# An attention and SwiGLU kernel on one core: a reordered opening, crossbar transposes of queries and keys from batch 2 on, values loaded uncast by SyncE, and one normalisation over two PSUM banks

## The chip, the cores and the metric

The kernel runs on one core of one Trainium2 chip. The metric is device time in microseconds (us), the median of several executions. The profile is one execution of the same program; its span is about two microseconds shorter than that execution's device time (424.5 us of 426.5 before).

Engines are named as in the profile: PE is TensorE, DVE VectorE, ACT ScalarE, POOL GpSimd (Pool), SP SyncE. "SPq" marks the time in which SyncE's sequencer is occupied with issuing a DMA.

## The reference, cut to what matters

```python
# q, k, v: (8 batches, 8 heads, 576 rows, 64); global_idx: 8 row numbers
scores = q @ k^T / sqrt(64)
mask   = (|i - j| <= 32) | row i is global | row j is global
x      = softmax(where(mask, scores, -1e9)) @ v       # -> (4608, 512)
g      = x @ w_gate                                   # (512, 1536)
out    = (g * sigmoid(g) * (x @ w_val)) @ w_out       # (4608, 512), float32
```

## The kernel before

The feed-forward part (FFN) works through nine chunks of 512 rows, which are numbered 0 to 8 here. A chunk is 12 gates (two PSUM tiles of four matmuls each, 128x512) and four output steps of 12 matmuls: 144 matmuls. The attention of batch c+1 is cut into steps that are issued between the gates of chunk c. So batch 0 runs alone at the start, chunks 0 to 6 carry the attention of batches 1 to 7, and chunks 7 and 8 are bare.

Four parts matter here. First, every batch's queries and keys are transposed by TensorE through PSUM and copied out by ACT and DVE. (Cuts are marked `...`.)

```python
def step_T(hp):                       # four of these per batch
    ...
    for name in ("k", "q"):
        ps = pm.tile([P, LJ, LP], BF16, tag="m", name="ps_t")     # pm: 2 tiles of one bank
        for j in range(LJ):
            for par in range(2):
                nc.tensor.transpose(out=ps[64*par : 64*par+64, j, :], ...)
        if name == "k": nc.scalar.copy(out=kT[:, hp, ...], in_=...)
        else:           nc.vector.tensor_copy(out=st["qT"][:, hp, :]..., in_=...)
```

Second, the values. Pool's DMAs cast them from float32 to bfloat16 on the way into `va`. SyncE then copies them within SBUF into `vb`, a version shifted by 64 rows, which half of the matmuls of the attention's second product ("AV") read.

```python
def load_v(b):
    for u in range(5):
        ...
        nc.gpsimd.dma_start(out=va[lo:hi, u, :, 0:D], in_=vs[t0 + lo : t0 + hi])

def load_vb(b):
    vb = bp.tile([P, 4, H, W], BF16, tag="vb", name="vb")
    nc.sync.dma_start(out=vb[0:64], in_=va[64:128, 0:4])
    nc.sync.dma_start(out=vb[64:128], in_=va[0:64, 1:5])
```

Third, the AV tiles: each pair of row tiles has two head groups, and each head group is one PSUM tile that DVE normalises by itself.

```python
def step_AV(u):
    for tp in (t0 // 2, t0 // 2 + 1):
        ps = pm.tile([P, 4, W], FP32, tag="m", name="ps_av")
        ...                                            # 10 matmuls, va and vb in turn
        normalise(ps, st["xa", tp][:, 4*hg : 4*hg+4, :])   # reduce, reciprocal, multiply
```

Fourth, the order. The gathered global rows are masked by Pool into `kqm` (`gather`, `gather_mask`); `kqm` is transposed by `step_GT`. The loop ties one attention step to each FFN unit, and the loads of batch c+2 to the third gate of chunk c.

```python
[L(step_T, 0), L(step_GT)], [L(step_T, 1)], [L(step_T, 2), vb], [L(step_T, 3)],
[L(step_S2)], [L(step_SG)], [L(step_P2T), L(step_S, 0)], [L(step_S, 1), L(step_AV2)],
[L(step_S, 2), L(step_AV, 0)], [L(step_S, 3), L(step_AV, 1)],
[L(step_X, 0), L(step_X, 1), L(step_S, 4)], [L(step_AV, 2)], [L(step_AV, 3)],
[L(step_X, 2), L(step_X, 3)], [L(step_AV8)], [L(step_X8)],
...
for c in range(NCH):
    steps = attention(c + 1) if c + 1 < B else []
    for i, f in enumerate(ffn(c)):
        f()
        for g in steps[i] ...: g()
        if i == 2 and c + 2 < B: prefetch(c + 2)     # gather, q and k, values, kqm
```

The softmax here doesn't subtract the row's maximum and nothing guards it: scores larger than these inputs give would overflow.

Of the kernel before, what the change touches and what calls it, by code (L numbers as in the profile page):

```python
# [26 lines left out]
def kernel(  # L27
# [22 lines left out]
    NCH = NT // CH  # L50
# [11 lines left out]
    ldp = ctx.enter_context(tc.tile_pool(name="ldp", bufs=2))  # L62
# [7 lines left out]
    pm = ctx.enter_context(tc.tile_pool(name="pm", bufs=2, space=bass.MemoryType.PSUM))  # L70
# [3 lines left out]
    def load_qk_part(b, tiles, hg):  # L74
        for name, src in (("k", k), ("q", q)):
            nc.gpsimd.dma_start(  # L76
                out=tiles[name][:, 4 * hg : 4 * hg + 4, :],
                in_=src[b, 4 * hg : 4 * hg + 4].rearrange("h (p j) d -> p h (j d)", j=LJ),
            )
# [6 lines left out]
    va_bufs = [const.tile([P, 5, H, W], BF16, name=f"va{i}") for i in range(2)]  # L86

    def load_v(b):
        va = va_bufs[b % 2]
        vs = v[b].rearrange("h s d -> s h d")  # L90
        for u in range(5):
            lo = WIN if u == 0 else 0
            hi = P - WIN if u == 4 else P
            t0 = P * u - WIN
            nc.gpsimd.dma_start(out=va[lo:hi, u, :, 0:D], in_=vs[t0 + lo : t0 + hi])  # L95

    def load_vb(b):
# [11 lines left out]
    load_qk_part(0, loaded[0], 0)  # L109
# [4 lines left out]
    iq_i = const.tile([P, KC], I32)  # L114
    nc.gpsimd.iota(iq_i, pattern=[[1, KC]], base=-WIN, channel_multiplier=0)
    load_qk_part(0, loaded[0], 1)
    i8_i = const.tile([P, NG], I32)
    nc.gpsimd.iota(i8_i, pattern=[[1, NG]], base=0, channel_multiplier=0)
    bofs_i = const.tile([P, B], I32)
    nc.gpsimd.iota(bofs_i, pattern=[[H * S, B]], base=0, channel_multiplier=0)  # L120
    band = const.tile([P, 64], BF16)
    nc.gpsimd.memset(band, 1.0)
    nc.gpsimd.affine_select(
        out=band, in_=band, compare_op=ALU.is_ge, fill=0.0,
        base=0, pattern=[[-1, 64]], channel_multiplier=1,
    )
    nc.gpsimd.affine_select(
        out=band, in_=band, compare_op=ALU.is_ge, fill=0.0,
        base=2 * WIN, pattern=[[1, 64]], channel_multiplier=-1,
    )  # L130
    for i in range(2):
        nc.gpsimd.memset(va_bufs[i][:, :, :, D : D + 2], 0.0)
        nc.gpsimd.memset(va_bufs[i][:, :, :, D : D + 1], 1.0)
        nc.gpsimd.memset(va_bufs[i][0:WIN, 0, :, :], 0.0)
        nc.gpsimd.memset(va_bufs[i][P - WIN : P, 4, :, :], 0.0)


    gidx_f = const.tile([P, NG], FP32)
    nc.vector.tensor_copy(
        out=gidx_f, in_=gidx_i64.bitcast(I32).rearrange("p (a b) -> p a b", b=2)[:, :, 0]  # L140
# [4 lines left out]
    )  # L145
    tmp8 = const.tile([P, NG], FP32)
# [3 lines left out]
    oh16 = const.tile([P, HP, 2, 2], FP32)  # L150
    nc.vector.tensor_reduce(
        out=oh16.rearrange("p h a r -> p (h a r)"),
        in_=ident.rearrange("p (a g) -> p a g", g=NG), axis=AX.X, op=ALU.add,
    )
    dmask = const.tile([P, HP, 2], FP32)
    nc.vector.tensor_tensor(out=dmask, in0=oh16[:, :, 0, :], in1=oh16[:, :, 1, :], op=ALU.add)
    mka = const.tile([P, 2, 2], FP32)
    nc.vector.tensor_reduce(
        out=mka, in_=oh16.rearrange("p h a r -> p a r h"), axis=AX.X, op=ALU.add
    )  # L160
    asel = const.tile([P, 2], FP32)
    nc.vector.tensor_reduce(out=asel, in_=mka, axis=AX.X, op=ALU.add)
    i8_f = const.tile([P, NG], FP32)
    nc.vector.tensor_copy(out=i8_f, in_=i8_i)
# [9 lines left out]
    bofs_f = const.tile([P, B], FP32)  # L174
    nc.vector.tensor_copy(out=bofs_f, in_=bofs_i)
    nc.vector.tensor_scalar(out=gofs, in0=bofs_f, scalar1=hrow, scalar2=None, op0=ALU.add)

# [21 lines left out]
    kqms = [None] * B  # L199
    g0 = gather(0)  # L200
    load_v(0)
    kqms[0] = gather_mask(*g0)

# [13 lines left out]
    for i in range(3):  # L217
        load_wgv(i)


    iq = const.tile([P, KC], FP32)
    nc.vector.tensor_copy(out=iq, in_=iq_i)
    nc.vector.tensor_scalar(out=iq, in0=iq, scalar1=gcol, scalar2=None, op0=ALU.subtract)
    m1 = const.tile([P, KC], BF16)
    nc.vector.tensor_scalar(out=m1, in0=iq, scalar1=0.0, scalar2=None, op0=ALU.is_equal)
    m0 = const.tile([P, KC], BF16)
    nc.vector.tensor_tensor(out=iq, in0=iq, in1=iq, op=ALU.mult)
    nc.vector.tensor_scalar(
        out=m0, in0=iq, scalar1=(WIN + 0.5) ** 2, scalar2=None, op0=ALU.is_gt
    )  # L230
    ones = const.tile([P, P], BF16)
    nc.vector.memset(ones, 1.0)
    ps_i = psc.tile([P, 2, 512], FP32, tag="sc", name="ps_i")
    for i in range(2):
        nc.tensor.matmul(
            out=ps_i[:, i, 0:320], lhsT=ones, rhs=m1[:, 320 * i : 320 * (i + 1)],
            start=True, stop=True,
        )
    mg = const.tile([P, S], BF16)
    mt = const.tile([P, KC], BF16)  # L240
    nc.vector.tensor_scalar(
        out=mg, in0=m0[:, WIN : WIN + S], scalar1=asel[:, 0:1], scalar2=None, op0=ALU.mult
    )
    nc.vector.scalar_tensor_tensor(
        out=mg, in0=m1[:, WIN : WIN + S], scalar=asel[:, 1:2], in1=mg,
        op0=ALU.mult, op1=ALU.add,
    )
    mg2 = const.tile([P, KC], BF16)
    nc.vector.scalar_tensor_tensor(
        out=mt.rearrange("p (i c) -> p i c", i=2), in0=ps_i[:, :, 0:320], scalar=0.5,  # L250
        in1=m0.rearrange("p (i c) -> p i c", i=2), op0=ALU.is_lt, op1=ALU.mult,
    )
    nc.vector.tensor_scalar(
        out=mt, in0=mt, scalar1=asel[:, 1:2], scalar2=None, op0=ALU.mult
    )
    nc.vector.memset(mt[:, 0:WIN], 0.0)
    nc.vector.memset(mt[:, WIN + S : KC], 0.0)
    nc.vector.scalar_tensor_tensor(
        out=mg2, in0=m1, scalar=asel[:, 0:1], in1=mt, op0=ALU.mult, op1=ALU.add,
    )  # L260

    kT_bufs = [const.tile([P, HP, KC], BF16, name=f"kT{i}") for i in range(2)]
    for i in range(2):
        nc.vector.memset(kT_bufs[i][:, :, 0:WIN], 0.0)
        nc.vector.memset(kT_bufs[i][:, :, WIN + S : KC], 0.0)


    def attention(b):
# [4 lines left out]

        def step_T(hp):
            if hp == 0:
                st["qT"] = bp.tile([P, HP, S], BF16, tag="qT", name="qT")
            for name in ("k", "q"):
                ps = pm.tile([P, LJ, LP], BF16, tag="m", name="ps_t")
# [8 lines left out]
                if name == "k":  # L287
                    nc.scalar.copy(  # L288
                        out=kT[:, hp, WIN : WIN + S].rearrange("p (i j) -> p i j", j=LJ),
                        in_=ps.rearrange("p j i -> p i j"),  # L290
                    )
                else:
                    nc.vector.tensor_copy(  # L293
                        out=st["qT"][:, hp, :].rearrange("p (i j) -> p i j", j=LJ),
                        in_=ps.rearrange("p j i -> p i j"),
                    )

        def step_GT():
            kqm = kqms[b]
            ps = pm.tile([P, 2, P], BF16, tag="m", name="ps_g")  # L300
# [8 lines left out]
        def step_SG():  # L309
            ps = psc.tile([P, 2, 512], FP32, tag="sc", name="ps_sg")  # L310
            for i in range(2):
                for hp in range(HP):
# [3 lines left out]
                        rhs=st["qT"][:, hp, 288 * i : 288 * (i + 1)],  # L316
# [28 lines left out]
        def step_P2T():  # L345
            ps = pm.tile([P, 5, P], BF16, tag="m", name="ps_p2t")
# [7 lines left out]
        def step_AV2():  # L354
            ps = pm.tile([P, 2, W], FP32, tag="m", name="ps_av2")
# [22 lines left out]
        def step_S(u):  # L378
# [6 lines left out]
            for slot, hp, t in slots:  # L385
                for par in range(2):
# [4 lines left out]
                        rhs=st["qT"][r : r + 64, hp, 64 * t : 64 * t + 64],  # L391
# [16 lines left out]
        def normalise(ps, xa):  # L408
            den = work.tile([P, 4], FP32, tag="den", name="den")
            nc.vector.tensor_reduce(  # L410
                out=den, in_=ps[:, :, D : D + 2], axis=AX.X, op=ALU.add
# [3 lines left out]
                out=xa, in0=ps[:, :, 0:D], in1=den.to_broadcast([P, 4, D]), op=ALU.mult  # L415
            )

        def step_AV(u):
            hg, t0 = ((0, 0), (1, 0), (0, 4), (1, 4))[u]
            pt = st["p", u]  # L420
            vb = st["vb"]
            for tp in (t0 // 2, t0 // 2 + 1):
                if hg == 0:
                    st["xa", tp] = work.tile([P, H, D], BF16, tag="xa", name="xa", bufs=4)
                ps = pm.tile([P, 4, W], FP32, tag="m", name="ps_av")
                for e in range(2):
                    nc.tensor.matmul(  # L427
                        out=ps[64 * e : 64 * e + 64],
# [3 lines left out]
                    )  # L432
                for hl in range(4):
                    for e in range(2):
                        slot = 4 * (hl // 2) + 2 * tp + e - t0
                        vv = va if e == 0 else vb
# [74 lines left out]
        ]  # L511


    def ffn(c):
        t0 = CH * c
        st = {}

# [51 lines left out]
    for s in attention(0):  # L569
        for f in s:  # L570
            f()
# [40 lines left out]
```

## Time and profile before

The time before is 424.86 us, the median of three executions (424.73 to 425.04).

These are lines of the page of the kernel before: busy time by engine, then the busy share of 40 equal slices in tenths (a 9 is 90% or more), then the TensorE clock in tenths and the DMA engines' busy share, then the engines' shares of the chain that ended last.

```profile
span 424.5 us, 9105 instructions
...
PE 377.0 (89%) x3788; PEld 192.4 (45%) x3850; DVE 266.2 (63%) x583; ACT 178.7 (42%) x281; POOL 92.7 (22%) x134
...
PE   0467888999989998999899989999999989999996
...
PEclk9999999999999999999999999999999999999999
DMA  7999999883537273647355726500030002002002
...
PE 69%; DVE 19%; ACT 5%; issue 3%; POOL 2%; DVEq 0%; ACTq 0%; POOLq 0%
```

TensorE is busy for 80% or more of every slice from the fifth to the last but one, the row shows its clock as full, and it holds 69% of the chain. The DMA engines are busy for 70% or more of each of the first eight slices, and far less later. So the kernel has a stretch at the start in which much data arrives, and after that it is bound by TensorE.

The next lines are TensorE's own timeline in the opening. The columns are start, duration, engine, line of the program, operation and operands; the bracket is the idle time before it and what ended it.

```profile
18.06 0.65 PE L302 MATMUL ps_g<-ident,kqm 128*128 128x128 bf16 x2 [5.82 <-POOL kqm L193]
...
43.95 1.49 PE L525 MATMUL pg<-xT,wg_sb 128*128 128x512 bf16 x3 [0.22 <-issue]
45.23 1.91 PE L525 MATMUL pv<-xT,wv_sb 128*128 128x512 bf16 x4
```

TensorE loses 5.82 us to Pool's masked global rows. (Before that, from the start to 10.43 us, it had waited for the tables that DVE computes.) The first FFN matmul is at 43.95 us. The clock's row may not be right for the opening: the four matmuls at 45.23 us take 1.91 us, where the next four of one gate, at 48.61 us, take 1.02.

These are lines of the same timeline in a steady chunk, which began at 180.54 us.

```profile
182.36 0.45 PE L282 MATMUL ps_t<-ident,k_bf 96*64 96x96 bf16 x12
182.64 0.42 PE L282 MATMUL ps_t<-ident,q_bf 96*64 96x96 bf16 x12
183.54 0.27 PE L302 MATMUL ps_g<-ident,kqm 128*128 128x128 bf16 x2 [0.48 <-ACT kT L288]
...
202.96 0.30 PE L427 MATMUL ps_av<-gvt,pg 128*64 128x264 bf16 x2 [0.26 <-DVE gvt L373]
...
209.17 0.40 PE L468 MATMUL ps_x<-ident,xa 128*128 128x128 bf16 x4 [0.47 <-DVE xa L414]
```

The first transposes of queries and keys start at 182.36 us, and the transpose of the global rows behind them waits 0.48 us for ACT's copy of the keys. The AV tiles wait for DVE twice (0.26 each, one shown) and the transposes of the normalised tile X wait twice (0.47, shown, and 0.35). That is 1.82 us of waiting in the chunk.

In SyncE's queue, batch 1's shifted values were issued at 51.21 and 51.80 us, well before TensorE came to them.

### The profile page before, as it was taken

What the parts mean: (1) busy time and instruction counts of PE and PEld (TensorE: products, weight loads), DVE (VectorE), ACT (ScalarE), POOL (GpSimd) and SP (SyncE); (2) the same over time, 40 slices, a digit from 0 to 9 for tenths busy, and PEclk for the clock granted to TensorE, in tenths of its full rate; (3) what the DMA queues carried; (4) which work ended last, traced back from release to release, by engine and by line L of the source; (5) the groups of instructions that cost most, each with busy time, mean ns of one, the idle gap of its engine ahead of it and who ended that gap; (6) DMA issues with size and microseconds to landing.
All of it is one profiled execution on the core that took longest, in us unless ns stands there. A gap on an engine that the chain in (4) does not pass through costs nothing.

```text
span 424.5 us, 9105 instructions
## 1 busy us (share of the span) xinstructions
PE 377.0 (89%) x3788; PEld 192.4 (45%) x3850; DVE 266.2 (63%) x583; ACT 178.7 (42%) x281; POOL 92.7 (22%) x134
## 2 busy tenths in 40 slices
PE   0467888999989998999899989999999989999996
PEld 0345444444544444454454445445444544444442
DVE  5456488727872788267845795488628882761760
ACT  1153255345643464256524653356245633323321
POOL 8942848232015101312113211100000000000000
PEclk9999999999999999999999999999999999999999
DMA  7999999883537273647355726500030002002002
GB/s 112 68 199 208 183 212 149 109 142 57 82 23 123 73 110 23 100 92 113 23 76 116 112 18 71 124 2 2 27 121 6 2 2 100 0 2 99 0 2 99
DMA packets 62234, 33.76 MB, mean 80 GB/s; under 512 B 39409, under 2 KB 56305, under 8 KB 62193
## 3 DMA queue, kind: packets, MB, share of 16 engines
q0 software_dynamic: 55584, 19.40, 40.6%
q1 hardware_dynamic: 6608, 13.77, 9.7%
q8 instruction: 30, 0.49, 0.5%
q14 instruction: 12, 0.09, 0.1%
HBM read 38.28 MB, written 9.44 MB: 112 GB/s over the span
## 4 chain that ended last, share of the span: by engine, by line
PE 69%; DVE 19%; ACT 5%; issue 3%; POOL 2%; DVEq 0%; ACTq 0%; POOLq 0%
PE po L541 22%; PE pg L525 17%; PE pv L525 16%; DVE pt L401 5%; PE ps_t L282 5%; DVE xa L414 3%; DVE h L536 3%; DVE gv L533 3%; ACT pe L396 3%; PE ps_x L468 2%; DVE den L413 2%; PE ps_av L427 1%; ACT kT L288 1%; DVE gvt L365 1%; PE ps_av L437 1%
## 5 line engine op out<-in xcount | busy, mean ns | idle before, releaser
L533 DVE SCALAR_TENSOR_TENSOR gv<-th,pg 128x512 bf16<-128x512 bf16 x108 | 74.0, 685 | 61.4 <-ACT th L531 54.4
L525 PE MATMUL pv<-xT,wv_sb 128*128 128x512 bf16 x418 | 109.7, 381 | 0.4
L525 PE MATMUL pg<-xT,wg_sb 128*128 128x512 bf16 x400 | 106.7, 382 | 3.4 <-issue 2.6
L541 PE MATMUL po<-wo_sb,h 128*128 128x512 bf16 x416 | 97.3, 380 | 0.8
L531 ACT ACTIVATE th<-pg 128x512 bf16<-128x512 f32 x108 | 64.5, 598 | 69.3 <-PE pg L525 65.0
L536 DVE TENSOR_TENSOR h<-gv,pv 128x512 bf16<-128x512 bf16 x108 | 74.3, 688 | 11.9 <-PE ps_s L388 0.5
L525 PEld LDWEIGHTS <-wv_sb 128*128 128x128 bf16 x432 | 42.5, 98 | 51.6 <-issue 1.1
L541 PEld LDWEIGHTS <-h 128*128 128x128 bf16 x432 | 40.2, 98 | 45.3
L95 POOL DMA_DIRECT2D va<-in_v_dram x40 | 33.8, 852 | 122.6 <-PE ps_av L437 90.4
L546 ACT ACTIVATE osb<-po 128x512 f32<-128x512 f32 x36 | 21.5, 597 | 89.5 <-PE po L541 89.5
L525 PEld LDWEIGHTS <-wg_sb 128*128 128x128 bf16 x432 | 36.1, 98 | 38.2 <-issue 4.1
L396 ACT ACTIVATE pe<-ps_s 128x1024 bf16<-128x1024 f32 (+1 forms) x40 | 37.6, 940 | 15.4 <-PE ps_s L388 13.9
L410 DVE TENSOR_REDUCE den<-ps_av 128x4 f32<-128x8 f32 x72 | 11.5, 159 | 41.1 <-PE ps_av L457 34.4
L288 ACT COPY kT<-ps_t 128x576 bf16<-128x576 bf16 x32 | 20.4, 638 | 36.8 <-PE ps_t L282 36.8
L401 DVE TENSOR_TENSOR pt<-pe,band 128x1024 bf16<-128x1024 bf16 (+1 forms) x40 | 25.4, 635 | 11.2 <-ACT pe L396 11.1
L414 DVE TENSOR_TENSOR xa<-ps_av,den 128x256 bf16<-128x256 f32 x72 | 30.6, 425 | 2.5
L293 DVE COPY qT<-ps_t 128x576 bf16<-128x576 bf16 x32 | 24.0, 750 | 4.5 <-PE ps_t L282 4.5
L427 PE MATMUL ps_av<-gvt,pg 128*64 128x264 bf16 x128 | 19.1, 305 | 6.3 <-DVE xa L414 3.3
L474 ACT COPY xT<-ps_x 128x512 bf16<-128x512 bf16 x32 | 18.0, 588 | 15.1 <-PE ps_x L468 15.1
L76 POOL DMA_DIRECT2D k_bf<-in_k_dram x16 | 11.8, 735 | 38.8 <-PE ps_t L282 35.5
L437 PEld LDWEIGHTS <-pt 128*64 128x64 bf16 x512 | 18.8, 117 | 0.3
L468 PE MATMUL ps_x<-ident,xa 128*128 128x128 bf16 x128 | 12.3, 231 | 7.5 <-DVE xa L414 7.2
(93 smaller groups left out, 286.6 us busy)
## 6 DMA issues: line engine op xcount, KB each, us to landing
out_dram<-osb SPq DMA_DIRECT2D x36, 256.0 KB, 2.0
k_bf<-in_k_dram POOLq DMA_DIRECT2D x16, 288.0 KB
q_bf<-in_q_dram POOLq DMA_DIRECT2D x16, 288.0 KB
vb<-va SPq DMA_DIRECT2D x16, 264.0 KB, 4.0
va<-in_v_dram POOLq DMA_DIRECT2D x24, 128.0 KB
va<-in_v_dram POOLq DMA_DIRECT2D x16, 96.0 KB
wg_sb<-in_moe_w_gate_dram POOLq DMA_DIRECT2D x3, 512.0 KB
wv_sb<-in_moe_w_val_dram POOLq DMA_DIRECT2D x3, 512.0 KB
```

The lines of the kernel that those rows point to most:

```text
L95: nc.gpsimd.dma_start(out=va[lo:hi, u, :, 0:D], in_=vs[t0 + lo : t0 + hi])
L288: nc.scalar.copy(out=kT[:, hp, WIN : WIN + S].rearrange("p (i j) -> p i j", j=LJ), in_=ps.rearrange("p j i -> p i j"),)
L293: nc.vector.tensor_copy(out=st["qT"][:, hp, :].rearrange("p (i j) -> p i j", j=LJ), in_=ps.rearrange("p j i -> p i j"),)
L396: nc.scalar.activation(out=pe, in_=ps[:, :, 0 : 64 * ns].rearrange("p r (s c) -> p r s c", c=64), func=AF.Exp, scale=SCALE,)
L401: nc.vector.tensor_tensor(out=pt.rearrange("p r s c -> p (r s) c"), in0=pe.rearrange("p r s c -> p (r s) c"), in1=bc(band, [[0, 2 * ns], [ ...
L414: nc.vector.tensor_tensor(out=xa, in0=ps[:, :, 0:D], in1=den.to_broadcast([P, 4, D]), op=ALU.mult)
L427: nc.tensor.matmul(out=ps[64 * e : 64 * e + 64], lhsT=st["pg"][:, P * tp + 64 * e : P * tp + 64 * e + 64], rhs=st["gv"].rearrange("p h r c ...
L525: nc.tensor.matmul(out=ps, lhsT=w[:, cc, P * fc : P * (fc + 1)], rhs=xT[:, cc, t0 : t0 + CH], start=(cc == 0), stop=(cc == NCC - 1),)
L531: nc.scalar.activation(out=th, in_=pg, func=AF.Tanh, scale=0.5)
L533: nc.vector.scalar_tensor_tensor(out=gv, in0=th, scalar=1.0, in1=pg, op0=ALU.add, op1=ALU.mult)
L536: nc.vector.tensor_tensor(out=st["h"][:, fc, :], in0=gv, in1=pv, op=ALU.mult)
L541: nc.tensor.matmul(out=po, lhsT=st["h"][:, fc, P * ts : P * (ts + 1)], rhs=wo_sb[:, fc, :], start=(fc == 0), stop=(fc == NFC - 1),)
```

## The change

The change means to shorten the opening and to take the query and key transposes off TensorE. It has five parts:

1. The opening is put in order of need: transposes first, the mask tables later, batch 0's tiles in the FFN's four PSUM banks, the last 64 rows of batch 0 deferred into chunk 0.
2. From batch 2 on, Pool casts queries and keys into DRAM (`kf`, `qf`), and SyncE's transposing DMA (through the crossbar) brings them into `kT` and `qT`.
3. SyncE loads the values as float32 into `vst`; Pool's cores cast them into `va`.
4. The two head groups of a row tile share one PSUM tile of two banks and one normalisation. This pool now has one buffer.
5. Attention steps are spread evenly over the FFN units by `interleave`; loads are tied to units by number.

```diff
-    pm = ctx.enter_context(tc.tile_pool(name="pm", bufs=2, space=bass.MemoryType.PSUM))
+    pm = ctx.enter_context(tc.tile_pool(name="pm", bufs=1, space=bass.MemoryType.PSUM))
 ...
     def load_v(b):
+            r.append(nc.sync.dma_start(out=vst[lo:hi, u], in_=vs[t0 + lo : t0 + hi]))
-            nc.gpsimd.dma_start(out=va[lo:hi, u, :, 0:D], in_=vs[t0 + lo : t0 + hi])
+    def cast_v(b, vst):
+                nc.gpsimd.tensor_copy(out=va[a:z, u, :, 0:D], in_=vst[a:z, u])
+    def cast_qk(b):
+            t = dram.tile([S, H, D], BF16, name=f"{name}f{b}")
+            nc.gpsimd.dma_start(out=t, in_=src[b].rearrange("h s d -> s h d"))
+    def transpose_qk(b):
+        nc.sync.dma_start_transpose(out=kT[:, :, WIN : WIN + S], in_=flat["k", b]...)
+        nc.sync.dma_start_transpose(out=qTs[b], in_=flat["q", b]...)
 ...                                   (order on Pool's queue in the opening)
+    load_wgv(0); load_wgv(1); loaded[1] = new_qk(); load_qk_part(1, ...) x2
+    load_wgv(2)
+    for i in range(4): nc.gpsimd.dma_start(out=wo_sb[...], ...)
+    kqms[1] = gather_mask(*gather(1))
 ...                                   (AV: both head groups, then one normalisation)
+        full = pm.tile([P, 2, 512], FP32, tag="m", name="ps_av")
+            for hg in range(2): ...
+            normalise(ps, st["xa", tp], 8)
 ...                                   (steps of batch 1 and of the later batches)
+        if b == 1:
+            head = [[L(step_T, 0)], [L(step_T, 1)], [L(step_T, 2), vb], [L(step_T, 3)], [L(step_GT)]]
+        else:
+            head = [[L(step_GT), vb]]
 ...
+    def interleave(units, steps):
+        for d, f in units:
+            f()
+            t += d
+            while i < len(steps) and (i + 0.5) * total <= t * len(steps):
+                for g in steps[i]: g()
+                i += 1
 ...
+    vsts[1], _ = load_v(1); cast_v(1, vsts[1]); cast_qk(2)      (after batch 0)
+            if c + 3 < B: at(1, cast_qk, c + 3)
+            at(3, transpose_qk, c + 2)
+            at(5, raw, c + 2)          # values of c + 2 by SyncE
+            at(6, rows, c + 2)         # gather and mask
+            at(9, lambda b: cast_v(b, vsts[b]), c + 2)
```

## The prediction

> **What bounds it now.** TensorE. In the page PE is 89% busy, DVE 63%, ACT 42%; in the chain that ended last PE holds 69%. The timeline shows three stages. Opening: the first FFN matmul starts at 43.95 us. Seven chunks with attention woven in: 47.6 us for the first, about 44.5 us for each of the others. Two bare chunks: 31.1 us each (144 matmuls at 0.216 us start to start), then a 3.8 us tail. So attention adds 13.3 us to a steady chunk. Read step by step as the gap between FFN matmuls, that is: transposes of q and k with the global rows 3.57 (0.48 of it waiting for an ACT eviction), scores and global parts 2.5, the eight AV tiles with scores 4.3 (0.52 waiting for DVE), X transposes 2.4 (0.82 waiting for the normalised tile), the rest 0.6.
>
> **Steady chunks (six, batches 2 to 7).** Removed from PE: 96 transposes, 4 x 0.72 us; from DVE 4 copies of 0.75, from ACT 4 of 0.64. Eight normalisations of 0.75 us (0.16+0.18+0.42) become four of about 1.05 (estimate: the 128x512 result at the 0.69 us that other 128x512 PSUM reads take). X now comes one unit after its AV tile, so most of its wait goes. But this PSUM pool has one two-bank tile in place of two: each tile waits for the eviction of the last. I expect AV0 to wait about 0.65 us for the global values, X0 and X1 about 0.3 each, AV8 behind X3 about 0.7. Sum: about 6.9 work + 1.9 to 2.5 waits, so a chunk of 40.2 us: 4.3 us less, 26 us over six. DVE and PE are both on this path; the evictions saved on ACT are not.
>
> **Opening.** PE today stands from 12.2 to 18.06 us until Pool masks the gathered rows, and 10.4 us until the mask tables. The new order puts four q/k transposes first, gives batch 0 four PSUM banks, and defers the last 64 rows. I expect the first FFN matmul at about 34 us, 10 us earlier.
>
> **What gives it back.** Weights still move at about 200 GB/s (wg 2 and wv 2 land at about 39.6 and 42.2 us, wo at 60.5, read from Pool's waits). The gather of batch 1 now queues behind wo, so its masked rows come at about 57 us; then its values are cast on Pool (six copies, about 3.6 us), then batch 2's q and k are cast DRAM to DRAM in 9,216 packets (about 10 us at v's packet rate of 14 ns per engine), and SyncE issues both crossbar transposes, which wait for that cast, before batch 1's shifted values. Those come at about 80 us, while PE wants them at about 66. All queues share the same 16 DMA engines (the Trainium skill, "DMA: Bandwidth & Descriptors", "Issuing engines are not separate DMA queues"). So chunk 0 stalls some 18 us in two places and ends at about 103 us, against 91.3 now: the opening's gain turns into a loss of 12 us.
>
> **Sum.** 103 + 6 x 40.2 + 62.2 + 3.8 = 410; I say 409, range 397 to 423. Faster by over 2%: 0.69; within: 0.26; slower: 0.05.
>
> **What would show it.** First FFN matmul near 34 us; a PE wait of 10 to 15 us at batch 1's first AV tile, ended by the DMA of the shifted values; chunks 1 to 6 near 40 us with no q/k transposes on PE; DMA share of these chunks about 0.6 to 0.7, from 0.52.
>
> **What would make it wrong.** Casts to DRAM with 128-byte writes, or transposes, far slower than v's packets: then the stall grows and chunks 1 to 6 wait for kT. Or a faster cast: no stall, about 395. Or DVE waiting for Pool's copies.

## The result, and the profile after

The changed kernel takes 434.6 us (433.27 to 435.29, four executions) against 424.8 us in the same rounds: a ratio of 1.0229, 95% interval 1.0202 to 1.0256. It is slower by 2.3%. All ratios in this document are the mean time of one kernel's fast runs over that of the other's fast runs of the same rounds, so they differ slightly from the ratio of the quoted medians.

The lengths of the stages, read from TensorE's timeline as the first FFN matmul of each chunk:

| stage, us | before | predicted | after |
|---|---|---|---|
| first FFN matmul at | 43.95 | about 34 | 34.78 |
| chunk 0 ends at | 91.61 | about 103 | 116.97 |
| chunks 1 to 6, mean of one | 44.46 | 40.2 | 41.37 |
| chunks 7 and 8, each | 31.08 | 31.1 | 31.08 |
| rest to the end of the span | 4.0 | 3.8 | 4.2 |

The opening and the bare chunks came as predicted. Chunk 0 took 82.19 us where 47.66 were needed before.

These are the page's lines of the kernel after.

```profile
span 431.6 us, 7877 instructions
...
PE 361.5 (84%) x3221; PEld 180.3 (42%) x3274; DVE 238.9 (55%) x467; ACT 161.8 (37%) x258; POOL 96.3 (22%) x122
...
PE   2668758028799989899899899898989998999996
...
PEclk9999979559999999999999999999999999999999
DMA  8999949998995939794989590168012001002002
```

TensorE does 15.5 us less and DVE 27.3 us less, yet the span is 7.1 us longer. The sixth, eighth and ninth slices of PE's row (5, 0 and 2, each slice 10.8 us) are the place. TensorE is idle in the eighth, and the clock's row shows its only dips there (7, then 5 and 5).

This is TensorE's timeline after, from the end of the opening to the end of chunk 0.

```profile
34.78 0.59 PE L604 MATMUL pg<-xT,wg_sb 128*128 128x512 bf16 x1 [0.67 <-ACT xT L541]
...
60.22 0.66 PE L366 MATMUL ps_g<-ident,kqm 128*128 128x128 bf16 x2 [3.58 <-POOL kqm L236]
...
63.59 1.91 PE L604 MATMUL pv<-xT,wv_sb 128*128 128x512 bf16 x4
...
73.84 0.19 PE L504 MATMUL ps_av<-va,pt 128*64 128x66 bf16 x1
93.98 0.21 PE L504 MATMUL ps_av<-vb,pt 128*64 128x66 bf16 x1 [19.95 <-DMA vb<-va]
...
116.97 0.81 PE L604 MATMUL pg<-xT,wg_sb 128*128 128x512 bf16 x3
```

The first wait is 3.58 us for `kqm`, the masked global rows of batch 1. The second is 19.95 us, in the middle of the first AV tile: the matmul that reads `va` has run, the next one reads `vb` and waits for its DMA. (A line gives the start of the first and the end of the last matmul of a group. Four gate matmuls take 1.03 us at full clock, and 1.91 us in the line of 63.59 us.)

This is SyncE's queue in the same stretch.

```profile
72.57 5.76 SPq L122 DMA_TRANSPOSE kT<-kf  x1
78.44 6.44 SPq L126 DMA_TRANSPOSE qT<-qf  x1
84.98 0.54 SPq L133 DMA_DIRECT2D vb<-va  x1
85.61 0.55 SPq L134 DMA_DIRECT2D vb<-va  x1
```

SyncE is occupied for 5.76 and 6.44 us with the two transposing DMAs, and only then issues the two halves of `vb`. TensorE wanted them at 74.0 us; they were issued at 84.98 and 85.61, and TensorE went on at 93.98.

This is Pool's timeline there.

```profile
59.77 0.39 POOL L236 TENSOR_TENSOR kqm<-kg,mka 128x128 bf16<-128x128 f32 x1 [13.50 <-DMA kg<-in_k_dram,gofs]
60.13 0.40 POOL L236 TENSOR_TENSOR kqm<-qg,mka 128x128 bf16<-128x128 f32 x1
60.59 3.85 POOL L108 CAST va<-vst 32x512 bf16<-32x512 f32 x6
64.39 2.28 POOL L115 DMA_DIRECT2D kf<-in_k_dram  x1
66.16 2.79 POOL L115 DMA_DIRECT2D qf<-in_q_dram  x1
```

Pool waits 13.50 us for the gather of the global rows, which is queued behind `wo`. Then it casts batch 1's values (3.85 us for six copies), and only then issues the casts of batch 2's queries and keys, which the transposes at 72.57 us wait for. From 67.88 us on it also issues the casts of batch 3, which then move while SyncE issues the transposes.

These are lines of the windows view of the kernel after, for the end of the stall and for a steady chunk; the last columns are the granted TensorE clock, the DMA share and GB/s. A steady chunk of the kernel before follows.

```profile
92.00:100.00 8.00, 5.30 (x67) 3.38 (x70) 2.87 (x6) 2.11 (x3) 3.19 (x6) 0.68 1.09 165
200.00:241.00 41.00, 38.34 (x359) 19.02 (x364) 25.98 (x50) 17.98 (x29) 11.34 (x12) 1.00 0.91 128
```

```profile
180.00:225.00 45.00, 42.45 (x461) 21.64 (x467) 29.84 (x66) 20.94 (x33) 10.36 (x14) 1.00 0.53 79
```

After the stall TensorE starts again at a reduced clock (0.68 on average from 92 to 100 us, of which the first 2 us still belong to the stall). In the steady chunk the DMA share rose from 0.53 to 0.91. The Trainium skill, "TensorE: Matmul & The Clock Gate", Part 1, says that the array falls to 4/8 of its clock after about one idle window of 3.4 us, and returns after about as long a busy time. The traces agree only roughly. After the wait of 3.58 us four gate matmuls take 1.91 us against 1.03, and the granted clock is back some 6 us after TensorE went on (at about 66.4 us); after the wait of 19.95 us it is back after about 3 (97.1). In the run e8 below it falls to half, from about 91.2 to 94.6 us, just after a wait of only 1.73 us.

These are the lines of a steady chunk after (it began at 199.94 us).

```profile
215.70 0.30 PE L495 MATMUL ps_av<-gvt,pg 128*64 128x264 bf16 x2 [1.08 <-DVE gvt L437]
...
218.12 0.40 PE L535 MATMUL ps_x<-ident,xa 128*128 128x128 bf16 x4
...
238.27 0.30 PE L516 MATMUL ps_av<-gvt,pg 128*64 128x264 bf16 x2 [0.94 <-ACT xT L541]
```

The transposes and their ACT wait are gone, and X no longer waits (218.12). There are new waits of 1.08 us at the first AV tile, for the global values that DVE computes, and of 0.94 us at the last, for ACT's copy of X: the price of one buffer in this pool.

### The profile page after: what moved, and what is told of

Same layout as the page of the kernel before. It is cut to its first block, busy times and chain, and to the rows that moved or that the text cites. A ratio compares the mean times of both kernels' runs of the same rounds, so it can differ in the third digit from the quotient of the medians.

```text
span 431.6 us, 7877 instructions
## 1 busy us (share of the span) xinstructions
PE 361.5 (84%) x3221; PEld 180.3 (42%) x3274; DVE 238.9 (55%) x467; ACT 161.8 (37%) x258; POOL 96.3 (22%) x122
## 5 line engine op out<-in xcount | busy, mean ns | idle before, releaser
L604 PE MATMUL pg<-xT,wg_sb 128*128 128x512 bf16 x402 | 109.9, 387 | 3.8 <-issue 2.2
L604 PE MATMUL pv<-xT,wv_sb 128*128 128x512 bf16 x425 | 111.8, 385 | 0.2
L623 PE MATMUL po<-wo_sb,h 128*128 128x512 bf16 x416 | 95.3, 379 | 2.2 <-issue 2.1
L108 POOL CAST va<-vst 128x512 bf16<-128x512 f32 (+3 forms) x48 | 31.2, 659 | 122.2 <-DMA vst<-in_v_dram 88.9
L604 PEld LDWEIGHTS <-wg_sb 128*128 128x128 bf16 x432 | 37.3, 99 | 42.5 <-issue 7.0
L477 DVE TENSOR_REDUCE den<-ps_av 128x8 f32<-128x16 f32 (+1 forms) x40 | 6.8, 170 | 60.0 <-PE ps_av L504 37.8
L504 PE MATMUL ps_av<-vb,pt 128*64 128x66 bf16 x256 | 18.6, 202 | 19.9 <-DMA vb<-va 19.9
L483 DVE TENSOR_TENSOR xa<-ps_av,den 128x512 bf16<-128x512 f32 (+1 forms) x40 | 25.5, 638 | 1.4
L504 PE MATMUL ps_av<-va,pt 128*64 128x66 bf16 x256 | 18.8, 202 | 0.0
L452 PE MATMUL ps_s<-qT,kT 64*128 64x64 bf16 x576 | 16.3, 197 | 1.8 <-DVE mg L311 1.0
```

The source lines that it names most:

```text
L108: nc.gpsimd.tensor_copy(out=va[a:z, u, :, 0:D], in_=vst[a:z, u])
L483: nc.vector.tensor_tensor(out=xa.rearrange("p (g h) d -> p g h d", g=g), in0=bc(ps, pst + [[1, D]]), in1=bc(den, [[4, g], [1, 4], [0, D]]) ...
L504: nc.tensor.matmul(out=ps[64 * e : 64 * e + 64, hg, hl, :], lhsT=pt[:, hl % 2, 4 * (hl // 2) + 2 * (tp % 2) + e, :], rhs=(va if e == 0 els ...
L604: nc.tensor.matmul(out=ps[:, 0:n], lhsT=w[:, cc, P * fc : P * (fc + 1)], rhs=xT[:, cc, t0 : t0 + n], start=(cc == 0), stop=(cc == NCC - 1),)
L623: nc.tensor.matmul(out=po, lhsT=st["h"][:, fc, P * ts : P * (ts + 1)], rhs=wo_sb[:, fc, :], start=(fc == 0), stop=(fc == NFC - 1),)
```

## The experiments

The theory at the start, the order theory: the 19.95 us wait comes from SyncE's queue, because the two transposes of batch 2 stand before the shifted values of batch 1 in program order. Its rival, the late-data theory: the wait comes from Pool's chain of gather, copy and cast, and the order on SyncE hardly matters. (The expectations give theories letters and say what each expects; F, which came up after e5, is that SyncE's queue holds back output stores as well.) Two smaller questions were what the joint normalisation costs, and what the crossbar is worth alone.

Stage lengths of all runs, read as above. "At" is the first FFN matmul.

| kernel | us (median) | ratio | at | chunk 0 | chunk 1 | chunks 2 to 6, mean |
|---|---|---|---|---|---|---|
| before | 424.8 | | 43.95 | 47.66 | 44.46 | 44.46 |
| after | 434.6 | 1.0229 | 34.78 | 82.19 | 41.19 | 41.40 |
| e1_vb_first | 417.22 | 0.9822 | 35.61 | 59.55 | 45.99 | 41.38 |
| e2_gather_early | 425.22 | 1.0014 | 36.81 | 72.15 | 41.23 | 41.49 |
| e3_both | 407.42 | 0.9593 | 35.60 | 55.33 | 40.92 | 41.45 |
| e4_crossbar_alone | 403.94 | 0.9510 | 43.96 | 45.68 | 40.98 | 40.98 |
| e5_one_bank | 406.83 | 0.9570 | 37.07 | 52.24 | 46.00 | 41.07 |
| e6_best | 425.31 | 1.0003 | 33.71 | 79.59 | 40.58 | 40.84 |
| e7_values_by_pool | 412.70 | 0.9720 | 35.74 | 65.20 | 40.57 | 40.58 |
| e8_pool_values_vb_first | 398.57 | 0.9350 | 36.86 | 49.50 | 44.46 | 40.57 |
| e9_sync_values_vb_first | 404.43 | 0.9502 | 33.97 | 49.96 | 48.43 | 40.78 |

Every kernel gave the reference's result.

### e1_vb_first: the order on SyncE alone

```diff
-            at(3, transpose_qk, c + 2)
+            at(5 if c == 0 else 3, transpose_qk, c + 2)
```

In chunk 0 there are 22 attention steps, and the shifted values are in the sixth. The interleaving puts that step after the fifth unit, and the transposes were tied to the fourth. Tied to the sixth, they come after the shifted values.

> Only change to the new kernel: on SyncE the two crossbar transposes of batch 2 are issued just after batch 1's shifted values (vb) instead of before them. Theory A (order on SyncE): vb of batch 1 is issued at about 64.5 us, right after Pool has cast the values, lands by about 71, and the 19.95 us wait of TensorE at batch 1's first AV tile shrinks to the 0.6 us for the global values; the time falls by about 20 us to about 414, faster than before. Rival B (traffic): the 16 DMA engines are full with casts from 67 us on, so vb is late whatever its place: the wait stays above 8 us and the time above 424. Rival C (the stall only moves): batch 2's first use of kT in chunk 1 now waits instead, and the time stays above 424.

Measured: 417.22 us, ratio 0.9822 (0.9806 to 0.9838). SyncE's queue of this kernel:

```profile
63.71 0.47 SPq L133 DMA_DIRECT2D vb<-va  x1
64.28 0.54 SPq L134 DMA_DIRECT2D vb<-va  x1
72.44 6.63 SPq L122 DMA_TRANSPOSE kT<-kf  x1
79.17 6.61 SPq L126 DMA_TRANSPOSE qT<-qf  x1
...
94.99 5.24 SPq L630 DMA_DIRECT2D out_dram<-osb  x4
```

The shifted values are issued at 63.71 us, 21.27 us earlier than after the change, though Pool's chain is where it was. The 19.95 us wait is gone: the first AV tile waits only 0.60 us, for the global values. The late-data theory falls for this wait. The gain is 17.4 us, less than the wait, because chunk 1 became 4.8 us longer. It begins with a wait of 3.36 us of TensorE at 100.19 us, which the profile puts down to ACT's copy of the last X tile. Pool had masked the global rows by 94.7 us, so it was not they. ACT itself was held up by an output tile:

```profile
99.28 0.60 ACT L628 ACTIVATE osb<-po 128x512 f32<-128x512 f32 x1 [7.72 <-DMA out_dram<-osb]
```

The eviction waited 7.72 us for an output store that frees its buffer, and SyncE issued that store only at 94.99 us, behind the two transposes and five value loads (85.95 us, 8.94 long). The half clock that followed (1.91 us for the four matmuls at 100.36 us) cost more. So e1 already shows the second effect of this queue, which e5 and e9 show again.

### e2_gather_early: the gather alone

```diff
     load_qk_part(1, loaded[1], 1)
+    g1 = gather(1)
     load_wgv(2)
 ...
-    kqms[1] = gather_mask(*gather(1))
+    kqms[1] = gather_mask(*g1)
```

> Only change to the new kernel: Pool issues the gather of batch 1's global rows ahead of the last gate/value weights and the output weights, and masks them where it did. Theory A: the wait at the global rows (3.58 us, and the half clock of the 4 us after it) goes, and Pool reaches the casts of values and of batch 2's q and k about 14 us earlier, at about 46 to 50 us; the casts then queue behind the output weights and land at about 62, so SyncE issues vb at about 74 to 76 instead of 85 and TensorE waits about 10 us instead of 20: about 420. If instead only the order on SyncE mattered, the wait for vb would stay near 20 us and the time above 430.

Measured: 425.22 us, ratio 1.0014 (0.998 to 1.0047). The wait for `kqm` is gone. The wait for the shifted values is still 14.38 us: the transposes go out earlier (64.02 us, against 72.57), but the shifted values still stand behind them and are issued at 76.38. Pool's chain thus shifts the queue, and the order within the queue makes the wait.

### e3_both

This is e1 and e2 together.

> Both of the above. Theory A: no long wait is left in chunk 0, which ends at about 91 us instead of 116.9, and chunks 1 to 8 are as in the new kernel (41.4 and 31.1 us): about 407. If the DMA engines' load were the limit (rival B), chunks 0 or 1 would show new waits of over 8 us and the time would stay above 415.

Measured: 407.42 us, ratio 0.9593 (0.9577 to 0.9609). No long wait is left, and the two repairs add up: 17.4 and 9.4 us alone, 27.2 together. So two changes of order, which take no work away, make of the slower kernel one that is 4.1% faster than the kernel before. What is left in chunk 0 are waits of at most 1.43 us, most of them at tiles of the one-buffer pool; two of them:

```profile
45.05 0.45 PE L347 MATMUL ps_t<-ident,q_bf 96*64 96x96 bf16 x12 [0.73 <-ACT kT L353]
...
81.12 0.40 PE L536 MATMUL ps_x<-ident,xa 128*128 128x128 bf16 x4 [1.26 <-DVE xa L484]
```

The X transpose at 81.12 us waits 1.26 us for the joint normalisation, and one more does. Earlier, where batch 1's queries and keys share a tile of the one-buffer pool, each of the four transpose steps waits 0.73 us for ACT's copy of the keys.

### e4_crossbar_alone: part 2 of the change, on the kernel before

```diff
+        if b < 2: (queries and keys loaded and transposed as before)
+        else:     cast_qk(b)
 ...
+            if i == 12 and c + 2 < B:
+                transpose_qk(c + 2)
```

> The kernel before, with only the crossbar part: q and k of batches 2 to 7 cast to DRAM by Pool and transposed by SyncE, placed behind that chunk's vb; opening, values and normalisation as before. If the crossbar part is worth what TensorE's transposes cost (4 x 0.72 us plus 0.48 us of waiting in each of six chunks), the steady chunk falls from 44.5 to about 41 us and the time to about 404; chunk 0 stays at about 47.6. If its DMA load gives that back (rival B), the chunks wait for kT or for values and the time stays above 415.

Measured: 403.94 us, ratio 0.951 (0.9494 to 0.9526). Each steady chunk falls from 44.46 to 40.98 us. This 3.48 us is more than the 2.88 us of TensorE transposes (four steps of 0.72), because the 0.48 us wait for ACT goes too. It is shorter than the changed kernel's steady chunk. So the crossbar gives the whole gain in the steady chunks, and something else in the change takes some of it back (e5 points to the joint normalisation). The transposes here stand behind the shifted values, at 81.41 us, where they delay nothing that an engine waits for (3.94 and 4.08 us of SyncE's time; three output stores stand behind them until 89.65 us, and ACT never waits for one).

### e5_one_bank: e3 without the joint normalisation

```diff
-    pm = ctx.enter_context(tc.tile_pool(name="pm", bufs=1, space=bass.MemoryType.PSUM))
+    pm = ctx.enter_context(tc.tile_pool(name="pm", bufs=2, space=bass.MemoryType.PSUM))
 ...
-            full = pm.tile([P, 2, 512], FP32, tag="m", name="ps_av")
             for hg in range(2):
+                ps = pm.tile([P, 4, W], FP32, tag="m", name="ps_av")
 ...
-            normalise(ps, st["xa", tp], 8)
+                normalise(ps, st["xa", tp][:, 4 * hg : 4 * hg + 4, :], 4)
```

Not shown: batch 1's transposes of queries and keys go back to one tile each, in place of a pair in one tile.

> The kernel with both mends (407.4 us), with one part of the change undone: one-bank tiles in two buffers in place of one two-bank tile, and each head group normalised by itself; the order of steps is kept. Theory D (the single two-bank buffer makes TensorE wait for the eviction it has just asked for): in chunk 0 the four waits of 0.73 us for kT inside the q/k transposes go, in the steady chunks the 0.94 us wait at the AV tile of the last 64 rows goes, so a steady chunk falls from 41.4 to about 40.4 and chunk 0 from 55.3 to about 52: about 398. Rival E (one normalisation in place of two is worth the 0.45 us of VectorE it saves per tile): the steady chunk gets longer, 42 us or more, and the time rises above 408.

Measured: 406.83 us, ratio 0.957 (0.9554 to 0.9586). This is a miss by about 9 us. The tiles did what was expected: chunk 0 is 3.1 us shorter than in e3 (the four waits of 0.73 us at batch 1's transposes are gone) and chunks 2 to 6 are 0.4 us shorter each. But chunk 1 grew to 46.0 us. In it, ACT waited 7.29 us to evict an output tile, because the output store that frees its buffer had not run. SyncE issued that store at 88.64 us, after the two transposes (66.90 and 73.61 us, 6.60 and 6.90 long) and five value loads (80.68, 7.86 long). This was the second effect of the same queue, on stores. (The half clock, from about 96.7 to 100.1 us, came on top.)

### e6_best: e5 with the AV steps grouped as in the kernel before

The label is what I hoped for; the kernel was not the best.

```diff
-            [L(step_AV, 0)], [L(step_X, 0), L(step_S, 2)], [L(step_AV, 1)],
-            [L(step_X, 1), L(step_S, 3)], [L(step_AV, 2)], [L(step_X, 2), L(step_S, 4)],
-            [L(step_AV, 3)], [L(step_X, 3)],
+            [L(step_S, 2), L(step_AV, 0)], [L(step_S, 3), L(step_AV, 1)],
+            [L(step_X, 0), L(step_X, 1), L(step_S, 4)], [L(step_AV, 2)],
+            [L(step_AV, 3)], [L(step_X, 2), L(step_X, 3)],
```

Not shown: in batch 1 the step of the global rows joins that of the last transposes, which takes away one more step.

> As the last, with the AV and X steps grouped as in the kernel before (two tiles of one head group per step, X of a pair after both), that is: opening in order of need with both mends, crossbar transposes, values by SyncE, no joint normalisation. If the opening's 8 us are real once its waits are mended, the first FFN matmul stays near 35.6 us, chunk 0 takes about 47 to 48 (45.7 in the crossbar-alone run plus three deferred steps), the steady chunks 41.0, and the time is about 396. If chunk 0 still takes 52 or more, the opening only moves work past the first FFN matmul, and the time is 400 or more, no better than the crossbar alone (403.9).

Measured: 425.31 us, ratio 1.0003 (0.9986 to 1.002). This is a miss by 29 us, and it repeats the first finding by accident. Chunk 0 now has 19 steps in place of 22, so the interleaving puts the sixth step after the sixth unit, behind the transposes and the value loads. SyncE's queue, and then the TensorE line that it delays:

```profile
65.05 5.67 SPq L122 DMA_TRANSPOSE kT<-kf  x1
70.83 6.83 SPq L126 DMA_TRANSPOSE qT<-qf  x1
77.89 8.23 SPq L100 DMA_DIRECT2D vst<-in_v_dram  x5
86.17 0.82 SPq L133 DMA_DIRECT2D vb<-va  x1
```

```profile
92.02 0.26 PE L504 MATMUL ps_av<-vb,pt 128*64 128x66 bf16 x1 [27.39 <-DMA vb<-va]
```

The wait is 27.39 us. No line about data was changed, only the number of steps in a table. The later chunks (40.58 to 41.3 us) are the shortest with SyncE's values so far.

### e7_values_by_pool: e6 with the values cast by Pool's DMA, as before

```diff
-            r.append(nc.sync.dma_start(out=vst[lo:hi, u], in_=vs[t0 + lo : t0 + hi]))
+            r.append(nc.gpsimd.dma_start(out=va[lo:hi, u, :, 0:D], in_=vs[t0 + lo : t0 + hi]))
```

> As the last, with the values part undone: Pool's queue loads and casts them in the DMA, as in the kernel before. The steady chunks should not change (41.0 both, since values arrive with a chunk to spare); in the opening the values land behind q and k on the one queue and Pool is free of 3.6 us of casts per batch. I expect within 3 us of the last run either way; a difference of over 5 us would show that the values' path is on the critical path of the opening.

Measured: 412.7 us, ratio 0.972 (0.9704 to 0.9737). This too was a miss: I expected no more than 3 us of difference from e6, and it was 12.6. The reason is the flaw that e6 carries. Without value loads on SyncE, the shifted values stand behind the two transposes only; they were issued at 71.84 us, and the wait was 14.70 us. The difference is in chunk 0, which is 14.4 us shorter; the first FFN matmul is 2.0 us later.

### e9_sync_values_vb_first and e8_pool_values_vb_first: the order mended, with the values on either engine

Both put the shifted values of batch 1 into the first step of chunk 0's transposes, where no step count can move them behind the crossbar's. e9 has the values on SyncE, e8 on Pool's DMA with batch 1's loads right after its gather.

```diff
-                [L(step_T, 0)], [L(step_T, 1)], [L(step_T, 2), vb], [L(step_T, 3), L(step_GT)],
+                [L(step_T, 0), vb], [L(step_T, 1)], [L(step_T, 2)], [L(step_T, 3), L(step_GT)],
 ...                                   (e8 only)
     g1 = gather(1)
+    vsts[1], _ = load_v(1)
     load_wgv(2)
```

> The 425.3 us run (opening, crossbar, values by SyncE, one-bank tiles) with only batch 1's vb moved one step earlier, in front of the transposes. Theory A: its 27.4 us wait goes and the time falls to about 398. Beyond that, if SyncE's queue is the limit (theory F: two transposes of 6 us and five value loads of 8 us hold back the output stores, whose three buffers fill and stop ScalarE), chunk 0 and 1 together stay 3 to 6 us longer than in the run with values by Pool, where SyncE issues no value loads; if the values' path does not matter, the two runs agree within 2 us.

> The values-by-Pool run (412.7 us) with batch 1's vb back in front of the transposes on SyncE, and batch 1's values loaded ahead of the last weights. Theory A (the place on SyncE again: there too the vb of batch 1 came behind the transposes, and TensorE waited 14.7 us for it): that wait goes, chunk 0 falls from 65.2 to about 49.5, the steady chunks stay 40.6: about 396. If the wait was the late values and not the order, TensorE still waits more than 5 us and the time stays above 402.

Measured: e9 takes 404.43 us, ratio 0.9502 (0.9487 to 0.9518); e8 takes 398.57 us, ratio 0.935 (0.9334 to 0.9365). Moving one call by two steps took e6's 27.39 us wait away and made it 20.9 us faster. Of the 5.9 us between e9 and e8 the two profiles show 2.6 (for e8 the slowest execution was profiled): e9 is 2.9 us ahead at the first FFN matmul, and loses 0.5 in chunk 0, 4.0 in chunk 1 (48.43 against 44.46) and 1.0 over chunks 2 to 6. Chunks 0 and 1 together are 4.4 us longer, as theory F expected; the 398 us expected of e9 were a miss by 6. In chunk 1 e9 repeats what e5 showed. SyncE's queue and ACT's line of e9:

```profile
65.60 5.93 SPq L122 DMA_TRANSPOSE kT<-kf  x1
71.64 7.07 SPq L126 DMA_TRANSPOSE qT<-qf  x1
78.88 8.67 SPq L100 DMA_DIRECT2D vst<-in_v_dram  x5
87.64 5.49 SPq L627 DMA_DIRECT2D out_dram<-osb  x4
```

```profile
92.18 0.60 ACT L625 ACTIVATE osb<-po 128x512 f32<-128x512 f32 x1 [11.11 <-DMA out_dram<-osb]
```

The store at 87.64 us stood behind 21.7 us of transposes and value loads (5.93 + 7.07 + 8.67). The eviction of the output tile at 92.18 us waited 11.11 us for it, and TensorE 4.84 us for the eviction. In e8 the transposes are issued at 63.37 and 69.22 us and the stores directly behind them, from 76.98 us on; ACT's evictions there wait only for TensorE.

e8 beats both kernels: 6.5% faster than before, 8.3% faster than the changed kernel (398.57 over 434.6, different rounds). In its profile, chunk 1 still opens with a wait for the global rows of batch 2:

```profile
89.98 0.59 PE L359 MATMUL ps_g<-ident,kqm 128*128 128x128 bf16 x2 [1.73 <-POOL kqm L232]
```

Its profiled execution was the slowest of its five (401.79 us; the others 397.38 to 399.7), so its stage lengths may be somewhat long. By this profile chunk 2 began at 130.82 us, against 130.62 in e4, whose opening is the old one. So the 7.1 us by which e8 was ahead at the first FFN matmul were used up by then. e8's other executions are up to 4.4 us faster than the profiled one, and where they keep this time was not seen. Two things point to the clock: in the profile four matmuls at 91.37 us, after the wait above, take 1.91 us in place of 1.03, and the mean granted clock was 0.994 in this execution, 0.996 to 1.000 in the others.

## Why the prediction was wrong

The prediction said 409 us with 5% for slower; it was 434.6 us. Its own sum was 410. Measured against it: chunk 0 ended 14.0 us later (116.97 against 103), six chunks cost 7.0 us more (41.37 against 40.2), and the rest (tail, and the median's distance from the profiled span) 3.6 us.

**Right: the opening.** "I expect the first FFN matmul at about 34 us": it was at 34.78.

**Right in mechanism: the two stalls.** The text named both places and both causes: the gather behind `wo` (predicted at about 57 us, Pool began the mask at 59.77), and the shifted values behind the transposes, which wait for the cast. It relied on the Trainium skill, "DMA: Bandwidth & Descriptors", "Issuing engines are not separate DMA queues", for the sharing of the 16 engines. The trace fits: the shifted values took 8.0 us to land in this stretch, with other DMAs in flight, and 4.0 us in the median of the whole run.

**The step that failed:** "SyncE issues both crossbar transposes, which wait for that cast, before batch 1's shifted values. Those come at about 80 us." The gather at 57, the copies of 3.6 and the cast of 10 put the transposes at 70.6, which leaves 9.4 us for both transposes and the flight of the shifted values. The trace has 72.57 for the first transpose. From there it took 12.4 us until the shifted values were issued (84.98), and 9.0 more until they landed (93.98): 21.4 us where 9.4 were allowed. With the 2.0 us of the later start, that is the whole 14.0 us. After the landing, 23.0 us to the end of chunk 0 were predicted and 23.0 measured. So the mis-sized term is the time that SyncE spends on issuing two transposing DMAs (12.2 us), and then the flight under load (9.0). The profile of before had no transposing DMA to read it from, and I put no figure to it. e1 shows that the order alone made the wait: with the transposes second, the same chain of Pool gave no wait there. I had listed transposes "far slower than v's packets" among what would make the prediction wrong, but with too little weight in the range.

That the last 23.0 us agree is partly luck, for the wait covered a second miss. The text had TensorE at the shifted values at about 66 us; it was there at 74.0. Without its two long waits chunk 0 took 58.7 us (82.19 - 3.58 - 19.95), where the prediction had about 51 (103 - 34 - 18). In e3, which has neither wait, chunk 0 took 55.33 us.

The traces also show with what the 12.2 us go together. While SyncE issued this pair, Pool's queue (the casts of batch 3 among them) moved 9754 packets; for the five later pairs of the same kernel it moved none, and each of these took 6.2 to 7.4 us of SyncE's time. So load on the DMA engines may have nearly doubled the term. This is read from the traces of the runs, and no experiment isolated it.

The Trainium skill describes how a DMA occupies its sequencer, and I did not use it. "Perfetto Trace Analysis", "DMA Instruction — HWDGE (DVE, Sync)", says that the sequencer is free for its next instruction only when all descriptors of a DMA have been generated, and that more descriptors may be made than the buffer holds. SyncE's lines here agree with the first: the next issue starts about 0.1 us after each transpose's 5.76 or 6.44 us. That the buffer is what makes them long, no run here shows.

**The steady chunks:** "about 6.9 work + 1.9 to 2.5 waits". The waits were 2.02 us in the chunk from 199.94 us (1.08 + 0.94), so their sum was right, though X waited not at all and the first AV tile longer than said. The work was 8.3 us (41.41 − 31.08 − 2.02). A plain subtraction would have given nearly that. Before, a steady chunk had 44.46 − 31.08 = 13.38 us of attention, 1.82 of it waits; without the 2.88 us of transposes, 8.7 us of work remain. The prediction's own list of steps gives the same 8.7 (3.57 + 2.5 + 4.3 + 2.4 + 0.6, less 2.88 and 1.82). One step that stayed can be compared: an AV step has 20 matmuls in both kernels and runs 0.61 us from its first matmul to the next FFN matmul (215.70 to 216.31, and 212.29 to 212.90 before).

**The joint normalisation** was counted as part of the gain. Between e3 and e5, which differ in it and its PSUM tiles alone, it costs about 0.4 us in each of chunks 2 to 6; whether by the lost second buffer or by the longer DVE pass, the two runs do not separate. The 3.1 us in chunk 0 are mostly not the normalisation: 2.9 of them are the four waits of 0.73 us at batch 1's shared tile of queries and keys.

**The DMA share** of chunks 1 to 6 was predicted at 0.6 to 0.7, from 0.52, and is 0.91 in the steady chunk shown. The casts and transposes fill the DMA engines more than I counted, but in these chunks they arrive in time: no TensorE wait there ends with a DMA.

**Not named at all:** that value loads and transposes also hold back output stores in SyncE's queue. In the changed kernel the long wait covers it; with the wait gone, it is the next limit (e1, e5, e9 against e8).

**Left open.** What sets the time of a transposing DMA on SyncE was not isolated by a run: it was 5.76 and 6.44 us in chunk 0, 4.03 and 3.15 in chunk 1 of the same kernel, and 3.94 and 4.08 in e4. Why e4's steady chunks are 0.4 us longer than e7's was not looked into either. And in no profile was the opening's gain of 9.2 us seen to last: e3 and e4 stand within 1.3 us of each other at the start of chunk 1 (90.93 and 89.64). The arrival of data is not the plain reason, though the DMA row is full until there: no wait of TensorE in chunk 0 of e3 ends with a DMA. TensorE is idle there for 9.8 us in all, 6.0 more than in chunk 0 of the kernel before (3.8), nearly all of it behind ACT and DVE, and chunk 0 is 7.7 us longer; the deferred rows are in it too. e8 and e9, without the shared tile, are still 3.3 and 5.7 us ahead of e4 at the start of chunk 1 (86.36 and 83.93), and lose it within chunk 1.

## What to carry to other kernels

When a change moves DMAs to another engine's queue, list the new queue in program order, give each entry its occupancy of the issuing sequencer, and ask what urgent small transfer or store stands behind a long one; this queue is not a dependency, so no wait of the old profile points to it. Where the position in that queue follows from a table of steps, pin the urgent transfer to an early step, since a mere change of the number of steps moved it here by 27 us of waiting. And for a part that stays, take the measured time and subtract what goes, rather than adding up steps anew.

## What the Trainium skill lacked or had wrong

- "DMA: Bandwidth & Descriptors", "Issuing engines are not separate DMA queues", says that the sequencer time to initiate a DMA "is usually small relative to the DMA itself". For the two transposing DMAs of 576 KB each here (576 x 512 in bfloat16) it was not: 5.76 and 6.44 us of SyncE's time, with 11.4 and 12.1 us from issue to landing. The page has no issue times by kind and size of DMA, measured on this chip; a table of them would have changed this prediction. Others from the changed kernel: 0.54 us for one half of the shifted values, 9.37 us for five strided float32 loads of values, 2.19 to 3.29 us of Pool for one cast of 576 KB to DRAM, and 0.74 us for a weight load.
- "Advanced Engine Details and Errata", "X-Bar Transpose (TRN2)", says "TRN2 transpose DMAs are as fast as regular DMAs". No run here compares the same bytes both ways. What the sentence leaves out, and the runs show, is the issuing queue: 12.2 us of SyncE for the pair in chunk 0 of the changed kernel, and 6.2 to 7.4 us for its later pairs.
- No page gives a time for a gather that stands behind other DMAs on Pool's queue. In the changed kernel Pool waited 13.50 us for one behind the output weights, and 16.71 us for one behind casts of queries and keys.
